# A transformer block's forward and backward: the DMA transposes replaced by TensorE transposes

## The chip, the cores and the metric

The kernel runs on one NeuronCore of a Trainium2 chip. A core has a matrix engine (TensorE, PE in the profile, with its weight loads listed as PEld), three engines for elementwise work (VectorE or DVE, ScalarE or ACT, GpSimd or POOL), and a queue engine for transfers (SyncE or SP). They run side by side, each in its own program order, and wait for each other by semaphores. Operands lie in SBUF, 128 partitions wide; TensorE writes its results to PSUM, from where DVE or ACT copies them out. The metric is the device time of one execution in microseconds; lower is better.

## What is computed

One transformer block with adaptive layer norm and all its gradients. S = 2048 tokens, D = 512, 32 heads of 16, a hidden layer of F = 1792; everything comes in and goes out as bf16.

```
mod = silu(c) @ w_mod                      -> sa, ca, ga, sb, cb, gb
h   = layernorm(x) * (1 + ca) + sa
q, k, v = split(h @ wqkv)                  32 heads of 16
x   = x + ga * (softmax(q k^T / 4) v) @ wo
h   = layernorm(x) * (1 + cb) + sb
out = x + gb * (relu(h @ w1 + b1)^2 @ w2 + b2)
...
returns out and the gradients of x, wqkv, wo, w1, b1, w2, b2, c, w_mod for grad_out
```

In the attention backward, for a head, with p the unnormalised exponentials of the transposed scores and dP the gradient that arrives at them, dS = p * dP. It is used twice: with its keys in the free dimension for dK (as it comes), and with its queries in the other place for dQ, which needs dS turned.

## The kernel before

**Stages.** `phase_fwd` (0 to 980 us) walks over four query chunks of 512, eight groups of four heads and two pairs of heads in each; a step is one block of 128 keys for one pair: two score matmuls into a PSUM tile of 1024 columns (L388), one exponential of it on ScalarE (L391), and eight small matmuls that multiply earlier exponentials with the values (L322). `last_chunk` (980 to 1166 us) does the output projection and the mlp of the last chunk and the weight gradients of the mlp (`gen_dw1`, `gen_dw2`). `phase5` with `attn_bwd` (1166 to 2376 us) is the attention backward, and `phase6` (to 2498 us) the gradients of wqkv, wo, x and the modulation.

**Background work in the forward.** Beside the steps runs other work, written as generators: `gen_qkv` projects q and k for the coming groups in the first chunk (one tile of 512 tokens of one group is a `gen_fm`), and from the second chunk on `gen_mlp` does everything that follows the attention of the chunk before: projection, layer norm, both mlp layers, their backward, and dO. A generator yields the cost of what it has issued, in units of a 512-column matmul. `Background.step` lets it run at a rate of 1.2 (first chunk) or 1.14 units a step; a yield of `("wait", n)` holds it for n steps, so that another engine or a transfer can finish. Some points must be reached by a deadline: `bg.until(mark)` runs the generator on without regard to rates or holds, for instance before a group's projections are needed, and at the end of the forward until the mark `fc2_2`. `bg.drain` does the same for what is left.

**Attention backward.** A unit is one block of 128 queries of one pair of heads (index `ib`, with `i = ib % 4`) against 512 keys (index `c`); there are 8 groups x 2 pairs x 4 x 16 = 1024. For each of the two heads of unit n the loop issues a score matmul (L1608, tile "st") and the dP matmul of unit n-1 (L1522, tile "dp"), the exponential (L1611, ScalarE), and dS = p * dP (L1526, VectorE). The score matmul and the dP matmul use different halves of the array's rows and run together. In 160 units the second half of dS goes over ScalarE and GpSimd instead (`dP_pool`, L1540 and L1541). Then come, in odd units, the four matmuls per unit of dK and dV (`kv`, L1459), and in even ones those of dQ (`dq`, L1484), which read dS turned. PSUM tiles come from pools: `stp` with three buffers for "st" (also for the turns), `dpp` with three for "dp". A new tile waits until the reader of the tile three before it in the same pool is done.

**The transposes before.** dS is collected for four units in a tile of 32 blocks of 128 x 128; after the fourth, SP issues one DMA transpose of it into a buffer `dsT` (L1549), and two such groups feed one round of `dq`. In one of four groups `turn_ds` (L1556 to L1566) turns the first four of the 32 blocks on TensorE instead. The same kind of transfer turns the projections into token-major form (L646), the values (L705), weights (L677, L1139, L1152, L1153), attention output and `grad_out` (L1176, L1178), the normalised input of the mlp (L1201), dx and dO (L1248, L1332), the mlp operands of the weight gradients (L946, L950), and dq, dk, dv in the tail (L1737). All are issued from SP and there are 416 of them.

Of the kernel before, what the change touches and what calls it, by code (L numbers as in the profile page):

```python
# [105 lines left out]
class K:  # L106
# [160 lines left out]
    def phase_fwd(self):  # L267
# [144 lines left out]
        self.gT_l = self.mk.tile([P, DT, 512], BF16, name="fT", bufs=2)  # L412
        nc.sync.dma_start_transpose(self.gT_l[:], self.io["grad_out"][0, S - 512:, :])
        x0s = []
# [209 lines left out]
    def gen_fm(self, ps, t, g, s0, dst=None, masked=None):  # L624
# [19 lines left out]
        def token_major():  # L644
            tm = eb.tile([P, 4, 4, 32], BF16, name="ev_tm")
            nc.sync.dma_start_transpose(tm[:].rearrange("p s j e -> p s (j e)"), dst)  # L646
            if t:
                nc.gpsimd.dma_start(self.ktm_d[g, :, s0:s0 + 512], tm[:].rearrange("p s j e -> p (s j e)"))
                return
            tmc = eb.tile([P, 4, 4, DH], BF16, name="ev_tmc")  # L650
            nc.gpsimd.tensor_copy(tmc[:], tm[:, :, :, 0:DH])
            w = 4 * DH
            nc.gpsimd.dma_start(self.qtm_d[g, :, s0 // P * w:(s0 // P + 4) * w],
                                tmc[:].rearrange("p s j d -> p (s j d)"))

        if self.late is None:
            token_major()
        else:
            self.late.append(token_major)
        yield 1  # L660

    def gen_qkv(self, kp):
# [3 lines left out]
        for g in range(1, NQ):  # L666
# [8 lines left out]
            if 3 < g <= 3 + self.DT:  # L675
                wt = self.qkv_eb.tile([P, 3 * self.DT, P], BF16, name="wm_t", bufs=1)
                nc.sync.dma_start_transpose(wt[:], w[:])  # L677
                nc.gpsimd.dma_start(self.WmT_d[g - 4], wt[:].rearrange("p n k -> p (n k)"))
# [14 lines left out]
    def gen_vt(self, s0):  # L693
# [4 lines left out]
        for k in range(4):  # L698
            vp = self.vpads[k]
            v = self.Vaug[:, s0 + k, :, 0:DH].rearrange("p (g j) d -> p g j d", j=4)  # L700
            one = self.qkv_eb.tile([P, 1], F32, name="one", bufs=2)
            nc.vector.memset(one[:], 1.0)
            nc.gpsimd.tensor_scalar(vp[:, :, 0:2, 0:DH], v[:, :, 2:4, :], one[:], 1.0, ALU.mult, ALU.mult)
            nc.gpsimd.tensor_scalar(vp[:, :, 2:4, 0:DH], v[:, :, 0:2, :], one[:], 1.0, ALU.mult, ALU.mult)
            nc.sync.dma_start_transpose(vT[:, :, k * P:(k + 1) * P], vp[:].rearrange("p g j e -> p (g j e)"))  # L705
            yield ("wait", 1)
        nc.gpsimd.dma_start(self.VTq_d.rearrange("g p s -> p g s")[:, :, s0 * P:(s0 + 4) * P], vT[:])

    def by_quad(self, t):
# [52 lines left out]
    def last_chunk(self, bg, O_b, x0s, o32):  # L762
# [10 lines left out]
        tm_v = lambda t: t.rearrange("(st p) d -> p st d", p=P)[:, st0:st0 + 4, :]  # L773
        tps = self.open_pool("tps", bufs=2, space=PSUM)
        e0 = self.open_pool("e0", bufs=1)
# [22 lines left out]
        for k in range(4):  # L798
            turn(O_b[:, k, :], DT, OT[:, k], "scalar" if k % 2 else "vector")
        bg.take(4)  # L800
        stats = mk.tile([P, 4, 6], F32, name="stats")
        mv = mk.tile([P, 4, 2], F32, name="mv")
# [136 lines left out]
    def turned(self):  # L939

        nc, ST, FT = self.nc, self.ST, self.FT
        lasts = []

        def get(pool, src, src_d, ft):
            r = pool.tile([P, ST - 4, P], BF16, name="tm_blk", bufs=4)
            nc.sync.dma_start_transpose(r[:], src_d[ft, :, :(ST - 4) * P])  # L946
            if ft % 4 == 0:
                n = min(4, FT - ft)
                t = pool.tile([P, 4, 4, P], BF16, name="tm_l", bufs=2)
                nc.sync.dma_start_transpose(t[:, :n].rearrange("p f s k -> p (f s) k"),  # L950
                                            src[:, ft:ft + n, :].rearrange("p f k -> p (f k)"))
                lasts.append(t)
            return [r[:, st, :] for st in range(ST - 4)] + [lasts[-1][:, ft % 4, i, :] for i in range(4)]

        return get

    def gen_dw1(self, sb, xh2, duT):
# [21 lines left out]

        dus = [turned(sb, duT, self.duT_d, ft) for ft in range(3)]  # L980
        for ft in range(2):
            load(ft)
        yield 0
        for ft in range(FT):
            if ft + 3 < FT:
                dus.append(turned(sb, duT, self.duT_d, ft + 3))
            if ft + 2 < FT:
# [36 lines left out]
    def gen_dw2(self, sb, g_tm, aT, tb):  # L1024
# [14 lines left out]
        mods = {2: (3, self.dsb_col), 5: (4, self.dcb_col)}  # L1039
        load(0)  # L1040
        load(1)
        yield 0
        load(2)
        for ft in range(FT):
            if ft + 3 < FT:
                load(ft + 3)
            a, w2_blk = blks[ft]
# [73 lines left out]
    def gen_weights_1(self):  # L1121
# [14 lines left out]
        for kt in range(DT):  # L1136
            nc.gpsimd.tensor_scalar(w1[:, kt, :], w1[:, kt, :], self.opcbT[:, kt:kt + 1], 1.0, ALU.mult, ALU.mult)
            yield 0
        nc.sync.dma_start_transpose(self.wogaT[:].rearrange("p a b c -> p (a b) c"), wo[:].rearrange("p a b -> p (a b)"))  # L1139

    def gen_weights_2(self):
# [4 lines left out]
        for (a, b) in zip(cuts, cuts[1:]):  # L1146
# [4 lines left out]
            yield ("wait", 4)  # L1151
        nc.sync.dma_start_transpose(self.W2gbT[:].rearrange("p a b c -> p (a b) c"), w2[:].rearrange("p a b -> p (a b)"))  # L1152
        nc.sync.dma_start_transpose(self.W1mT[:].rearrange("p a b c -> p (a b) c"), w1[:].rearrange("p a b -> p (a b)"))  # L1153
        yield ("wait", 8)
# [13 lines left out]
    def gen_mlp(self, sc, O_b):  # L1168
# [4 lines left out]
        tm_v = lambda t: t.rearrange("(st p) d -> p st d", p=P)[:, st0:st0 + 4, :]  # L1173
        x_v, g_v, out_v = tm_v(io["A_x"][0]), tm_v(io["grad_out"][0]), tm_v(io["out_0"][0])
        OT = mk.tile([P, 4, DT, P], BF16, name="fT", bufs=2)
        nc.sync.dma_start_transpose(OT[:].rearrange("p a b c -> p (a b) c"), O_b[:].rearrange("p a b -> p (a b)"))  # L1176
        gT = mk.tile([P, DT, 512], BF16, name="fT", bufs=2)
        nc.sync.dma_start_transpose(gT[:], io["grad_out"][0, s0:s0 + 512, :])  # L1178
        yield ("wait", 9 if sc else 14)
        x1 = mk.tile([P, 4, D], F32, name="x1")  # L1180
# [19 lines left out]
        xhT = mk.tile([P, 4, DT, P], BF16, name="fT", bufs=2)  # L1200
        nc.sync.dma_start_transpose(xhT[:].rearrange("p a b c -> p (a b) c"), xh[:].rearrange("p a b -> p (a b)"))  # L1201
        nc.gpsimd.dma_start(tm_v(self.xhat2_d), xh[:])
# [29 lines left out]
        for k in range(4):  # L1232
# [14 lines left out]
            dxT = mk.tile([P, DT, P], BF16, name="dxT", bufs=2)  # L1247
            nc.sync.dma_start_transpose(dxT[:], dxb[:])  # L1248
            todo.append((k, dxT))
# [39 lines left out]
    def gen_do(self, sc, k, dxT, pads=None, o32=None):  # L1289
# [41 lines left out]
        c0 = k % 2 * P  # L1331
        nc.sync.dma_start_transpose(self.dOTq[:, :, c0:c0 + P], dOpad[:].rearrange("p g j e -> p (g j e)"))  # L1332
        if k % 2:
# [97 lines left out]
    def attn_bwd(self):  # L1431
# [17 lines left out]
        masked, kvs = self.masked, self.kvs  # L1449
        pend, pendq, turnq, two = [], [], [], []  # L1450
        own = dT_free[-1]
# [91 lines left out]
        def dS(u):  # L1543

            (T, g, jp, c, ib, kvT, pu, dsg, i, grp) = u
            pend.append((T, g, jp, c, ib, kvT, pu, dsg[:, i]))
            if i == G - 1:
                dsT, n = grp
                nc.sync.dma_start_transpose(dsT.rearrange("p (b k) -> p b k", k=P)[:, n:, :],  # L1549
                                            dsg[:].rearrange("p i a k -> p (i a k)")[:, n * P:])  # L1550
                two.append(dsT)
                if len(two) == 2:
                    pendq.extend((T, g, jp, c, ib - 2 * G + 1, a, sub, two[:]) for a in range(2) for sub in range(4))
                    two.clear()

        def turn_ds(dsg, grp, skip, late):  # L1556

            dsT = next(t for t in dT_free if not late or t is not own)
            dT_free[:] = [t for t in dT_free if t is not dsT]
            grp.extend((dsT, 0 if skip else 4))  # L1560
            if skip:
                return
            tp = stp.tile([P, 4, P], BF16, name="st")
            for b in range(4):
                nc.tensor.transpose(tp[:, b, :], dsg[:, 0, 0, b * P:(b + 1) * P], self.ident[:])
            nc.scalar.copy(dsT[:, 0:4 * P], tp[:].rearrange("p b k -> p (b k)"))  # L1566

# [4 lines left out]
        for g in range(NQ):  # L1572
            for jp in range(2):
# [16 lines left out]
                for c in range(SC):  # L1590
                    c0 = 512 * c
                    for ib0 in range(0, ST, G):
# [6 lines left out]
                        for i in range(G):  # L1599
# [19 lines left out]
                            if i % 2 == 1 and len(pend) >= 4:  # L1619
                                kv_two(1 if odd(c, ib) else 2)  # L1620
                            elif i % 2 == 0 and len(pendq) > 2 * G:
                                for _ in range(4 if end else 2):
                                    dq(pendq.pop(0))
                            if i == 2:
                                turn_ds(dsg, grp, no_turn(c, ib), end and m > 2)
            T = Tn
        with tc.manual_schedule(engines=ALL):
# [3 lines left out]
            for a in range(2):  # L1631
                dP(last, a)
            dS(last)
            while len(pend) > 2:
                kv_two()
# [49 lines left out]
    def phase6(self):  # L1685
# [47 lines left out]
        def load_a(i):  # L1733
            s2 = order[2 * i]
            dqT = wk.tile([P, 3, 2, DT, P], BF16, name="dqT", bufs=3)
            for t in (1, 2, 0):
                nc.sync.dma_start_transpose(dqT[:, t].rearrange("p s n k -> p (s n) k"),  # L1737
                                            parts[t][:, s2:s2 + 2, :].rearrange("p s d -> p (s d)"))
            dx1s = [wk.tile([P, D], F32, name="dx1_6", bufs=6) for _ in range(2)]
# [226 lines left out]
```

## Time and profile before

| | us |
|---|---|
| time, median of 3 runs | 2512.6 (2509.9 to 2517.3) |
| profiled execution, its own time | 2500.3 |
| its span | 2498.5 |

The page's first two lines of totals, and its row of the span in 40 slices, where a digit is the busy share in tenths and PEclk the clock that TensorE was granted:

```profile
PE 2410.2 (96%) x26211; PEld 1061.6 (42%) x26439; DVE 1695.0 (68%) x3487; ACT 2283.1 (91%) x3757; POOL 753.5 (30%) x1337
## 2 busy tenths in 40 slices
PE   8999999999999999999999999999999999999998
PEld 4555555555555555583233332333333333333343
DVE  6222322422332343576999999999999999999957
ACT  7999999999999997534999999999999999999945
POOL 2344531220131022245222323322333222322223
PEclk9999999999999999999999999999999999999999
DMA  4589661541243045499999999999999999999997
```

A busy TensorE is not one at its peak, since the ends of its matmuls are modelled; what bounds a stage has to be read from that stage. The forward is slices 1 to 15, the last chunk 16 to 18, the attention backward 19 to 38. A row of the page's groups gives the line, the engine, what is written and read with its shape, the count, then busy time and mean duration of one (ns), and the idle time just before it with what ended it.

### The profile page before, as it was taken

The page shows a single profiled execution, that of the slowest core. Times are in us where ns is not written, and L with a number is a line of the kernel's source. Part 1 is how long each engine was busy: PE and PEld are TensorE (multiplying, and loading weights), DVE is VectorE, ACT ScalarE, POOL GpSimd, SP SyncE. Part 2 cuts the span into 40 slices and gives each one's busy share as a digit, 9 for nine tenths or more (in the row PEclk, how much of TensorE's full clock was granted, in tenths as well). Part 3 has the DMA queues.
Part 4 walks back from the last instruction along what each step waited for, and adds up shares of the span by engine and source line. Part 5 has one row for each costly group of instructions (what it writes and reads, how often), then busy time and mean ns, then how long its engine had stood idle before and what let it go on. Part 6 is the DMA issues. An engine that isn't in the chain of part 4 may idle for free.

```text
span 2498.5 us, 67897 instructions
## 1 busy us (share of the span) xinstructions
PE 2410.2 (96%) x26211; PEld 1061.6 (42%) x26439; DVE 1695.0 (68%) x3487; ACT 2283.1 (91%) x3757; POOL 753.5 (30%) x1337
## 2 busy tenths in 40 slices
PE   8999999999999999999999999999999999999998
PEld 4555555555555555583233332333333333333343
DVE  6222322422332343576999999999999999999957
ACT  7999999999999997534999999999999999999945
POOL 2344531220131022245222323322333222322223
PEclk9999999999999999999999999999999999999999
DMA  4589661541243045499999999999999999999997
GB/s 166 135 179 208 169 125 47 132 100 40 92 114 98 23 123 147 110 199 216 232 235 233 232 227 231 237 234 231 230 235 239 234 230 236 234 233 236 238 217 192
DMA packets 1293547, 454.13 MB, mean 182 GB/s; under 512 B 1236948, under 2 KB 1261398, under 8 KB 1293222
## 3 DMA queue, kind: packets, MB, share of 16 engines
q1 hardware_dynamic: 1252422, 344.68, 71.8%
q0 software_dynamic: 38720, 104.04, 13.9%
q8 instruction: 207, 3.39, 0.6%
q10 hardware_dynamic: 2080, 1.05, 0.2%
q14 instruction: 118, 0.97, 0.1%
HBM read 75.83 MB, written 64.49 MB: 56 GB/s over the span
## 4 chain that ended last, share of the span: by engine, by line
PE 49%; ACT 35%; DMA 7%; issue 5%; DVE 3%; POOL 1%; SPq 1%; ACTq 0%; DVEq 0%; POOLq 0%
ACT pu L391 26%; PE st L1608 17%; PE acckv L1459 8%; ACT pu L1611 6%; DMA dsT<-ds 5%; PE accq L1484 5%; PE st L388 4%; PE dp L1522 2%; PE accbank L322 2%; PE dps L1050 2%; PE dp L1659 1%; PE st L1754 1%; ACT csq L1540 1%; PE pps L1237 1%; DVE ds L1526 1%
## 5 line engine op out<-in xcount | busy, mean ns | idle before, releaser
L1526 DVE TENSOR_TENSOR ds<-dp,pu 128x512 bf16<-128x512 f32 x1888 | 1166.0, 682 | 34.6 <-PE dp L1522 19.1
L1611 ACT ACTIVATE pu<-st 128x512 bf16<-128x512 f32 x2048 | 1073.8, 666 | 34.7 <-PE st L1608 21.3
L391 ACT ACTIVATE pu<-st 128x1024 bf16<-128x1024 f32 x992 | 912.1, 1077 | 4.2 <-PE st L388 3.7
L388 PE MATMUL st<-QTm,KTq 128*128 128x512 bf16 x1859 | 560.9, 377 | 27.1 <-ACT pu L391 6.1
L322 PEld LDWEIGHTS <-pu 128*128 128x128 bf16 x8192 | 346.7, 96 | 236.1 <-issue 3.0
L1522 PE MATMUL dp<-kvm,q 64*128 64x512 bf16 x1024 | 365.0, 384 | 2.0 <-DVE ds L1526 0.7
L322 PE MATMUL accbank<-Vaug,pu 128*128 128x17 bf16 x8192 | 357.4, 171 | 8.3 <-ACT Vaug L522 1.1
L1522 PE MATMUL dp<-kvm,dOTg 64*128 64x512 bf16 x1024 | 363.6, 383 | 0.3
L1608 PE MATMUL st<-kvm,q 64*128 64x512 bf16 x1024 | 349.4, 382 | 5.4 <-ACT pu L1611 0.2
L1608 PE MATMUL st<-kvm,QTg 64*128 64x512 bf16 x1024 | 348.1, 381 | 6.5
L1541 POOL TENSOR_TENSOR ds<-csq,pu 128x512 bf16<-128x512 f32 x128 | 147.2, 1150 | 627.0 <-ACT csq L1540 553.6
L388 PEld LDWEIGHTS <-KTq 128*128 128x128 bf16 x1984 | 188.4, 96 | 176.9 <-issue 124.8
L1459 PE MATMUL acckv<-ds,Qg 128*16 128x512 bf16 x1024 | 176.2, 382 | 0.3
L1459 PE MATMUL acckv<-pu,q 128*16 128x512 bf16 x1024 | 176.3, 383 | 0.0
L1459 PE MATMUL acckv<-ds,q 128*16 128x512 bf16 x1024 | 176.2, 383 | 0.0
L1459 PE MATMUL acckv<-pu,dOg 128*16 128x512 bf16 x1024 | 176.0, 382 | 0.0
L302 POOL DMA_DIRECT2D QTm<-QTq_d x124 | 63.1, 511 | 341.5 <-PE st L388 320.0
L1608 PEld LDWEIGHTS <-q 64*128 64x128 bf16 x1024 | 67.0, 94 | 163.5 <-issue 150.6
L1608 PEld LDWEIGHTS <-QTg 64*128 64x128 bf16 x1024 | 67.1, 94 | 160.6 <-issue 145.7
L329 DVE RECIPROCAL rl<-accbank 128x4 f32<-128x4 f32 x128 | 22.9, 179 | 158.3 <-PE accbank L322 158.2
L1522 PEld LDWEIGHTS <-q 64*128 64x128 bf16 x1024 | 88.8, 93 | 52.9 <-issue 43.3
L1522 PEld LDWEIGHTS <-dOTg 64*128 64x128 bf16 x1024 | 88.2, 93 | 52.9 <-issue 43.8
(390 smaller groups left out, 3055.1 us busy)
## 6 DMA issues: line engine op xcount, KB each, us to landing
KTq<-KTq_d POOLq DMA_DIRECT2D x24, 512.0 KB, 3.9
duT_d<-auT POOLq DMA_DIRECT2D x3, 1792.0 KB, 7.9
aT_d<-rT POOLq DMA_DIRECT2D x3, 1792.0 KB, 11.5
KTq_d<-KTq SPq DMA_DIRECT2D x32, 128.0 KB, 2.1
QTq_d<-ev_fm SPq DMA_DIRECT2D x32, 128.0 KB, 4.3
ktm_d<-ev_tm POOLq DMA_DIRECT2D x32, 128.0 KB, 2.5
VTq_d<-vT POOLq DMA_DIRECT2D x4, 1024.0 KB, 6.3
dx<-dx_d SPq DMA_DIRECT2D x16, 256.0 KB, 4.6
```

What stands on the lines that cost most here:

```text
L302: nc.gpsimd.dma_start(QTm[j][32 * j:32 * j + 32, :], self.QTq_d[g, 32 * j:32 * j + 32, 512 * qc:512 * (qc + 1)])
L322: nc.tensor.matmul(acc[:, a, sub, :], lhsT=pu[:, a, sub * P:(sub + 1) * P], rhs=Vaug[:, kb, h, :], start=(kb == 0 and a == 0 and sub == 0) ...
L388: nc.tensor.matmul(stt[:, a, :], lhsT=KT[:, kb * P:(kb + 1) * P], rhs=QTm[2 * jp + a][:], start=True, stop=True)
L391: nc.scalar.activation(pu[:], stt[:], ACT.Exp, scale=self.scale)
L1050: nc.tensor.matmul(pt[:], lhsT=a[st], rhs=g_tm[:, st, :], start=(st == 0), stop=(st == ST - 1))
L1459: nc.tensor.matmul(acckv[r:r + DH, :], lhsT=T[n][:, ib, col:col + DH], rhs=src[:, a, :], start=(ib == 0), stop=(ib == ST - 1))
L1484: nc.tensor.matmul(accq[r:r + 32, o:o + 256], lhsT=T["K"][:, 4 * c + sub, col:col + 32], rhs=v[:, r // 32 % 2 * 2:r // 32 % 2 * 2 + 2, 4 * ...
L1522: nc.tensor.matmul(dp[:], lhsT=T["dOT"][rd, ib * P:(ib + 1) * P], rhs=masked["VT"][a][rd, 512 * c:512 * (c + 1)], start=True, stop=True)
L1526: nc.vector.tensor_tensor(dsg[:, i, a], dp[:], pu[:, a, :], ALU.mult)
L1541: nc.gpsimd.tensor_tensor(dsg[:, i, 1], f[:], pu[:, 1, :], ALU.mult)
L1608: nc.tensor.matmul(stt[:], lhsT=T["QT"][rs, q], rhs=masked["KT"][a][rs, c0:c0 + 512], start=True, stop=True)
L1611: nc.scalar.activation(pu[:, a, :], stt[:], ACT.Exp, scale=self.scale)
```

## The change

Every DMA transpose is replaced by transposes on TensorE: the block is loaded as the stationary operand, the identity streams past it, the result lands in PSUM in bf16, eight blocks of 128 x 128 to a PSUM tile, and is copied to its place in SBUF. A helper `gen_turn` does this, with a yield of 1.5 units after four blocks and after each tile; `turn_now` is the same without yields. The copies are made by VectorE where nothing else is said, and by ScalarE and VectorE in turn for dS, for the weight gradients' operands and for dq, dk, dv.

- dS: each unit is turned by itself, eight blocks, one unit after its dS was issued (`turn_unit`); the PSUM tile is an "st" tile of the pool `stp`, the copy is ScalarE's for even `i`, VectorE's for odd. `turn_ds` goes, and dQ starts one group earlier (`len(pendq) > G`).
- Forward: `gen_fm`, `gen_vt`, `gen_qkv`, `gen_mlp`, `gen_do`, `gen_weights_1` and `gen_weights_2` turn through `gen_turn` with tiles of the pool `mps`, and get holds in front of the turns in which an operand is not ready at once.
- Weight gradients: the operands come by a plain transfer into one staging buffer (`tm_st`), and are turned at the next request.
- `grad_out` is loaded plainly and turned from SBUF; in the last chunk it is turned by `last_chunk`'s own `turn`.

```diff
-            nc.sync.dma_start_transpose(tm[:].rearrange("p s j e -> p s (j e)"), dst)
+            self.turn_now(tm[:].rearrange("p s j e -> p s (j e)"), dst, 4)
...
-        if self.late is None:
-            token_major()
-        else:
+        if self.late is not None:
             self.late.append(token_major)
-        yield 1
+            yield 1
+            return
+        yield ("wait", 1)
+        token_major()
+        yield 1.5
...
+    def gen_turn(self, dst, src, n, pool=None, name="pps", copies=None):
+
+        nc = self.nc
+        for b0 in range(0, n, 8):
+            m = min(8, n - b0)
+            pt = (pool or self.mps).tile([P, 8, P], BF16, name=name)
+            for i in range(m):
+                nc.tensor.transpose(pt[:, i, :], src[:, (b0 + i) * P:(b0 + i + 1) * P], self.ident[:])
+                if i == 3:
+                    yield 1.5
+            (copies or [nc.vector.tensor_copy])[b0 // 8 % len(copies or [0])](dst[:, b0:b0 + m, :], pt[:, :m, :])
+            yield 1.5
+
+    def turn_now(self, *a, **k):
+        for _ in self.gen_turn(*a, **k):
+            pass
...
         def get(pool, src, src_d, ft):
-            r = pool.tile([P, ST - 4, P], BF16, name="tm_blk", bufs=4)
-            nc.sync.dma_start_transpose(r[:], src_d[ft, :, :(ST - 4) * P])
+            flush()
+            g = pool.tile([P, (ST - 4) * P], BF16, name="tm_st", bufs=1)
+            nc.sync.dma_start(g[:], src_d[ft, :, :(ST - 4) * P])
+            r = pool.tile([P, ST - 4, P], BF16, name="tm_blk", bufs=3)
+            todo.append((r[:], g[:], ST - 4))
...
         xhT = mk.tile([P, 4, DT, P], BF16, name="fT", bufs=2)
-        nc.sync.dma_start_transpose(xhT[:].rearrange("p a b c -> p (a b) c"), xh[:].rearrange("p a b -> p (a b)"))
+        yield ("wait", 3)
+        yield from self.gen_turn(xhT[:].rearrange("p a b c -> p (a b) c"), xh[:].rearrange("p a b -> p (a b)"), 4 * DT)
...
             dxT = mk.tile([P, DT, P], BF16, name="dxT", bufs=2)
-            nc.sync.dma_start_transpose(dxT[:], dxb[:])
+            yield ("wait", 3)
+            yield from self.gen_turn(dxT[:], dxb[:], DT)
...
-        nc.sync.dma_start_transpose(self.dOTq[:, :, c0:c0 + P], dOpad[:].rearrange("p g j e -> p (g j e)"))
+        yield ("wait", 4)
+        yield from self.gen_turn(self.dOTq[:, :, c0:c0 + P], dOpad[:].rearrange("p g j e -> p (g j e)"), NQ)
...
             pend.append((T, g, jp, c, ib, kvT, pu, dsg[:, i]))
+            tq.append(u)
+
+        def turn_unit(u):
+
+            (T, g, jp, c, ib, kvT, pu, dsg, i, grp) = u
+            if not grp:
+                late = (g, jp) == (NQ - 1, 1) and c * SC + ib // G > 2
+                grp.append(next(t for t in dT_free if not late or t is not own))
+                dT_free[:] = [t for t in dT_free if t is not grp[0]]
+            dsT = grp[0]
+            self.turn_now(dsT.rearrange("p (b k) -> p b k", k=P)[:, 2 * G * i:2 * G * (i + 1), :],
+                          dsg[:, i].rearrange("p a k -> p (a k)"), 2 * G, pool=stp, name="st",
+                          copies=[(nc.scalar.copy, nc.vector.tensor_copy)[i % 2]])
             if i == G - 1:
-                dsT, n = grp
-                nc.sync.dma_start_transpose(dsT.rearrange("p (b k) -> p b k", k=P)[:, n:, :],
-                                            dsg[:].rearrange("p i a k -> p (i a k)")[:, n * P:])
                 two.append(dsT)
...
-                            elif i % 2 == 0 and len(pendq) > 2 * G:
+                            elif i % 2 == 0 and len(pendq) > G:
                                 for _ in range(4 if end else 2):
                                     dq(pendq.pop(0))
-                            if i == 2:
-                                turn_ds(dsg, grp, no_turn(c, ib), end and m > 2)
+                            while len(tq) > 1:
+                                turn_unit(tq.pop(0))
...
             for t in (1, 2, 0):
-                nc.sync.dma_start_transpose(dqT[:, t].rearrange("p s n k -> p (s n) k"),
-                                            parts[t][:, s2:s2 + 2, :].rearrange("p s d -> p (s d)"))
+                self.turn_now(dqT[:, t].rearrange("p s n k -> p (s n) k"), parts[t][:, s2:s2 + 2, :].rearrange("p s d -> p (s d)"),
+                              2 * DT, pool=stp, name="st", copies=[(nc.scalar.copy, nc.vector.tensor_copy)[t % 2]])
```

## The prediction

> **What bounds the kernel now.** I read the table of stretches first, then the costliest groups, then the transposes that TensorE (PE) already makes, last the timeline. The stretches (columns: stretch, its length, busy us and instructions of PE, PEld, DVE, ACT, POOL, granted PE clock, DMA share, GB/s) are opening, forward, last chunk, backward loop and tail:
>
> ```profile
> 64.00:301.00 237.00, 223.02 (x2774) 129.04 (x2822) 61.12 (x160) 235.29 (x257) 107.98 (x192) 1.00 0.76 177
> 301.00:980.00 679.00, 656.23 (x8027) 370.88 (x8176) 217.05 (x646) 676.48 (x738) 150.67 (x242) 1.00 0.36 91
> 980.00:1166.50 186.50, 177.09 (x1539) 111.43 (x1547) 117.01 (x463) 73.30 (x171) 80.70 (x118) 0.99 0.79 184
> 1166.50:2376.00 1209.50, 1187.38 (x12772) 371.30 (x12772) 1174.66 (x1904) 1194.02 (x2427) 355.64 (x680) 1.00 1.20 232
> 2376.00:2498.50 122.50, 111.10 (x596) 49.80 (x603) 83.16 (x208) 56.33 (x114) 39.32 (x69) 0.98 0.86 205
> ```
>
> In the forward ACT alone is full. In the backward loop ACT (99%), PE (98%) and DVE (97%) all are, and so are the DMA engines (share 1.20); only POOL has room. The loop is 1024 units in 1209.5 us, 1.18 us each. Its work per unit, from the groups:
>
> ```profile
> L1526 DVE TENSOR_TENSOR ds<-dp,pu 128x512 bf16<-128x512 f32 x1888 | 1166.0, 682 | 34.6 <-PE dp L1522 19.1
> L1611 ACT ACTIVATE pu<-st 128x512 bf16<-128x512 f32 x2048 | 1073.8, 666 | 34.7 <-PE st L1608 21.3
> ```
>
> The idle before each is small: nobody waits long. The removed operation, in the view of its line, issues 256 transfers, 7.2 us each to land, and is waited for by PE 8.5 us in 1209.5:
>
> ```profile
> L1549 SPq DMA_TRANSPOSE dsT<-ds x208: 3490/4262/6457, 1173.4 to 2377.8; - x104
> L1549 SPq DMA_TRANSPOSE keep<-ds x48: 3550/4204/5392, 1192.2 to 2300.7; - x48
> ...
>   PE accq L1484: 8.5, 13
> ```
>
> So the change takes nearly nothing off the path, and puts its work on the engines that are full.
>
> **Prices.** The trace has PE transposes with both kinds of copy (tile view of last_chunk's turn; min/median/max in ns):
>
> ```profile
> L782 PE MATMUL tp<-ident,dOpad x32: 219/219/229, 1039.9 to 1061.0; 128*128 128x128 bf16 x32
> L783 DVE COPY fT<-tp x4: 414/418/424, 983.2 to 997.6; 128x512 bf16<-128x512 bf16 x4
> ...
> L783 ACT COPY dOTq<-tp x4: 1003/1012/1012, 1040.8 to 1061.3; 128x1024 bf16<-128x1024 bf16 x4
> ```
>
> And it has the loop's own four-block turn among its neighbours:
>
> ```profile
> 1606.05 0.38 PE L1608 MATMUL st<-kvm,q 64*128 64x512 bf16 x1
> ...
> 1606.44 0.29 PE L1484 MATMUL accq<-dsT,keep 128*32 128x256 bf16 x2
> ...
> 1606.78 0.40 PE L1565 MATMUL st<-ident,ds 128*128 128x128 bf16 x4
> ...
> 1607.11 0.39 PE L1608 MATMUL st<-kvm,q 64*128 64x512 bf16 x1
> ...
> 1607.22 0.62 ACT L1566 COPY dsT<-st 128x512 bf16<-128x512 bf16 x1
> ...
> 1607.69 1.13 ACT L1611 ACTIVATE pu<-st 128x512 bf16<-128x512 f32 x2
> ```
>
> Four transposes take 0.40 us of which 0.22 is the last one's length, so they start 0.06 apart (in the records 0.056); start to the next matmul, with the change of array tiling, is 0.33. Eight take 0.33 + 4 x 0.056 = 0.55, from first start to end 0.62. The exponentials of 512 columns follow each other at 0.48 (two in 1.13, the last being 0.65), so ACT's slot is 0.48 for 512 columns; for 1024 I take 0.91, the pace of the forward's L391 (912.1 us / 992 = 0.92). DVE's copy of 1024 bf16 is in no row: from 418 ns for 512 (about 0.15 fixed, the rest 1.9 columns a ns) 0.69 us.
>
> Two rules of the Trainium skill stand against rows. "TensorE: Matmul & The Clock Gate", Part 4: PE-mode transpose, gives some 275 ns per transpose inside a kernel and says it does not count toward releasing the clock. By that 8 would cost 2.2 us a unit, the loop 1.8 ms more; the records' 0.056 us between starts makes it 0.45. The 219 ns are latency, and the clock stayed at 1.00 in the loop, though with few transposes. I take the row. "VectorE: DVE Perf Modes", Rules for kernel authors, tells one to accept 1x on PSUM sources; its cycle table then makes 1024 columns 1.19 us (estimate). The 418 ns for 512 are below 1x, so 0.69 it is; 1.19 is kept as a rival.
>
> **Backward loop.** The built program has 8,192 PE transposes of dS, eight per unit, and 1024 copies of 1024 columns, 512 on ACT (even units), 512 on DVE. Work per pair of units: PE 1.9 to 2.2 (its matmuls in the timeline) + 2 x 0.55 = 3.0 to 3.3; ACT 4 x 0.48 + 0.91 = 2.83 and its small copies; DVE 4 x 0.60 + 0.65 = 3.05, less what POOL takes.
>
> That is not yet the pace. Pool stp has three PSUM buffers and each unit now draws three tiles (st, st, turn), so each buffer gets a fixed job and PE loses its lead on ACT: the second st of unit n+1 waits for the second exponential of unit n, and a turn for the copy of the turn before it. On ACT the even copy stands before the next unit's two exponentials. The ring over two units: second st of an even unit to dq 0.31; dq to first transpose 0.33; eight transposes 0.62; to the copy 0.06; copy 0.91; exponential 0.48; second exponential to its end 0.63; to the next even unit's second st 0.05 (PE follows ACT at that distance in the forward). Sum **3.39 us a pair**, longer than any engine's work; ACT stands idle some 0.5 of it. The DVE copy fits: it starts 3.06 after the ring's start and ends at 3.75, the turn that waits for it is due at 4.0.
>
> 512 x 3.39 = 1736. Added: 160 units send half their dS through ACT and POOL (1150 ns each, L1541), which now must end before that unit's turn, +0.31 each, 50; 48 turns of dk, dv and dq, 0.7 each, 33; 64 kvT copies, mostly in ACT's idle, 10. Sum 1829. My hand sums fall short of the real loop: for before, ACT's rows give 1149 (977 exponentials, 77 + 36 + 31 + 28 copies) where 1209.5 passed, 5%. I add half of that, 48. Loop 1877, **+667**.
>
> **Forward.** It keeps to ACT's 0.917 us a step while the background stays within its rate. Each projection tile now costs a hold and half a unit more, and in the first query chunk no longer fits: the program forces the rest out between steps, eleven blocks in the built order: four of four or five tiles, seven of about two. A forced tile is 4 matmuls (0.65 to the last start), 1.18 to the end of its DVE cast (0.38 + 0.06 + 0.69 + 0.05), 0.22 for four transposes: 2.05 with ACT idle. 4 x 9.4 + 7 x 3.7 less the 3 that before has: **+60**. In the later chunks the turns (48 units and 31 held steps each) make the mlp late by about 67 of 256 steps a chunk, so that nearly all of chunk 2's mlp is left at the last step and runs with no exponential beside it: first layer 56 x 0.216 = 12.1, xhT 1.8; du 14 x 1.05 by DVE = 14.7 + 1; then four tiles with their norm chain on DVE, which was hidden:
>
> ```profile
> 942.92 0.70 DVE L1273 BATCH_NORM_STATS2 lnd_st<-pps 128x6 f32<-128x512 f32 x1 [3.20 <-PE pps L1237]
> ...
> 946.17 0.43 DVE L1244 CAST dxb<-dx 128x512 bf16<-128x512 f32 x1
> ```
>
> The last matmul started at 942.51 and the cast ends at 946.60: 4.1, of which PE waits 3.9. A tile: 3.0 + 3.9 + 0.2 = 7.2; its dO, 0.86 + 3.5 (DVE, 946.59 to 949.83) + 0.45 = 4.8. 4 x (7.2 + 4.8) + fc2 3.2 = 51. Sum 81 less before's 2: **+79**. Norm chains that outlast their holds: about 4, left out.
>
> **Last chunk and tail.** 448 transposes of the weight gradients at 0.056 in a stretch where PE is the bound: 25; their loads now go through one staging buffer: 3.9 us to landing (row for 512 KB) against 3.6 + 0.7 of PE a tile, so hidden; 23 fc2 units more, 5; gT 1: **+31**. Tail: 192 transposes, 11, and changes 2; the last dS transfer (12.5 us in the chain of waits) goes, of which I count 6, for other matmuls lie beside it: **+7**. W2gbT, W1mT and woga: PE work within the forward's rate, counted in its lateness.
>
> Sum: 667 + 60 + 79 + 31 + 7 = 844 on the profiled execution's 2500.3: 3344. The median of the runs shown is 12 higher, so **3350 us**, 33% slower.
>
> **Rivals.** (1) *The engines overlap fully*: queues absorb the ring, and the loop goes at ACT's work: 1149 - 31 + 466 = 1584, times 1.05: 1667, +458; 3150. For it: ACT is 99% busy in before with the same order of work. Against it: three tiles on three buffers. (2) *DVE's copy at 1x*: 1.19 us ends at 4.25, the even turn slips 0.28 a pair, and DVE's work becomes 3.6 a pair: 512 x 0.3 = 150; 3500. (3) *Transposes at 275 ns or a gated clock*: 9,680 x 0.22 = 2100; 5450. (4) *Not slower*: the dS transfers are the bound, not the engines; the chain of waits has them at 5% (125 us), the DMA share is 1.20, and without them 2500 - 125 = 2375. It decides only if ACT's added work per unit stays below its idle, 1.2% of 1.18 us or 0.015, against 0.45 added; and PE's measured wait is 8.5, not 125. (5) *The change doesn't do this*: excluded by the built order, where SP has no transposes left.
>
> **Chances.** Mine 0.75; (1) 0.13; (2) 0.09; (3) 0.02; (4) 0.01. Mine alone is 3240 to 3470 (ring 3.2 to 3.6). The range reaches (1) and beyond (2): 3140 to 3560. A change of 0.3% is about what can be told from none here; faster 0.01, same 0.01, slower 0.98.
>
> **What would show it.** Loop length near 1880 with ACT below 90% busy and its idle ended by PE's turns; PE's st waiting for ACT; the DVE copy at 0.69; DMA share far below 1; eleven gaps in ACT before 310 us, and some 80 us after the last exponential of the forward with DVE and PE taking turns. Wrong if ACT stays at 97% or more (rival 1), the copies differ, or transposes start more than 0.06 apart.

## The result and the profile after

The changed kernel takes **3308.9 us** (median of 4 runs, 3305.1 to 3313.3) where the kernel before took 2511.2 on the same chip (4 runs, 2507.2 to 2517.3): a ratio of 1.317, interval 1.314 to 1.321. The profiled execution's span is 3303.3 us, 804.8 more than before.

The table of stretches of the changed kernel, with the columns of the prediction's first table: the first chunk from 64 us, the later chunks to the last exponential of the forward (at 1043.7), a new stretch behind it, the last chunk, the backward loop from its first to its last exponential, and the tail:

```profile
64.00:301.00 237.00, 198.31 (x2444) 117.94 (x2485) 79.29 (x199) 174.15 (x189) 78.11 (x147) 1.00 0.23 75
301.00:1043.70 742.70, 703.82 (x8909) 415.60 (x9072) 215.26 (x611) 737.84 (x805) 158.45 (x253) 1.00 0.21 67
1043.70:1138.50 94.80, 62.43 (x285) 27.16 (x286) 60.25 (x154) 1.06 (x2) 20.68 (x33) 0.82 0.29 93
1138.50:1367.30 228.80, 208.77 (x2001) 138.22 (x2013) 129.57 (x495) 109.57 (x209) 80.71 (x119) 0.99 0.43 136
1367.30:3163.00 1795.70, 1747.64 (x20708) 830.55 (x20707) 1540.83 (x2414) 1688.87 (x2873) 357.45 (x680) 1.00 0.05 13
3163.00:3303.30 140.30, 124.77 (x787) 61.88 (x795) 89.61 (x218) 72.27 (x131) 38.78 (x69) 0.97 0.38 121
```

Four things are to be seen. In the first chunk ACT is busy 174 of 237 us, 235 before. The third row is work that had hardly existed as a stretch of its own: ACT busy 1 us of 95, PE and DVE 62 and 60, so they take turns, and the granted clock falls to 0.82. In the loop the DMA share is 0.05 (1.20 before), all three engines have more to do, and DVE is no longer full (86%). In the tail nothing but the length stands out.

By the same boundaries in both traces, the stages account for all of it. The profiled execution of before was 11 us faster than its median, so the profiles are 805 us apart and the medians 798.

| stage | before | after | more | forecast |
|---|---|---|---|---|
| forward, to its last exponential | 979.5 | 1043.7 | 64 | 60 |
| from there to the last chunk | 2.8 | 94.9 | 92 | 79 |
| last chunk, to the loop's first exponential | 184.6 | 228.7 | 44 | 31 |
| loop, first to last exponential | 1208.9 | 1795.9 | 587 | 667 |
| tail | 122.6 | 140.1 | 17 | 7 |
| sum | | | 805 | 844 |

The waits of the first chunk (64 to 301 us), and those of the stretch behind the forward; after the waiting engine and line and what it waited for: us, times, longest:

```profile
ACT pu L391 <- PE st L388: 61.3, 12, 10.5
```

```profile
PE pps L717 <- DVE dxb L1278: 16.4, 4, 5.1
PE pps L717 <- DVE dOpad L1360: 13.7, 4, 3.4
```

Ten of the 12 waits are forced projection blocks (the other two are 0.5 us each), and an eleventh block follows at 304.5 us: in the trace the distance of two exponentials is 9.1 us once, 11.6 three times and 4.3 to 4.8 seven times, where a step takes 0.92. The eight waits of 3.4 to 5.1 us are the norm chain and the dO chain of the third chunk's mlp, each now with a turn at its end for which PE waits.

### The profile page after: what moved, and what is told of

The parts are those of the page before. It is cut to its first block, busy times and chain, and to the rows that moved or that the text cites. A ratio compares the mean times of both kernels' runs of the same rounds, so it can differ in the third digit from the quotient of the medians.

```text
span 3303.3 us, 86819 instructions
## 1 busy us (share of the span) xinstructions
PE 3101.7 (94%) x35635; PEld 1620.8 (49%) x35879; DVE 2156.8 (65%) x4195; ACT 2831.5 (86%) x4259; POOL 753.4 (23%) x1337
## 4 chain that ended last, share of the span: by engine, by line
PE 50%; ACT 35%; issue 10%; DVE 3%; DMA 1%; POOL 1%; ACTq 0%; POOLq 0%; DVEq 0%; SPq 0%
ACT pu L391 21%; PE st L717 13%; PE st L1642 12%; ACT pu L1645 8%; PE accq L1520 4%; PE acckv L1495 4%; ACT dsT L720 3%; PE st L388 3%; PE accbank L322 1%; PE st L1790 1%; PE pps L630 1%; PE dp L1695 1%; PE dps L1080 1%; PE dps L1024 1%; ACT csq L1576 1%
## 5 line engine op out<-in xcount | busy, mean ns | idle before, releaser
L1562 DVE TENSOR_TENSOR ds<-dp,pu 128x512 bf16<-128x512 f32 x1888 | 1228.6, 685 | 203.3 <-PE dp L1558 155.3
L1645 ACT ACTIVATE pu<-st 128x512 bf16<-128x512 f32 x2048 | 1127.1, 611 | 53.1 <-PE dp L1558 17.0
L717 PE MATMUL st<-ident,ds 128*128 128x128 bf16 x8192 | 645.8, 220 | 17.6 <-ACT dsT L720 3.1
L717 PEld LDWEIGHTS <-ds 128*128 128x128 bf16 x8192 | 487.1, 97 | 303.5 <-issue 266.0
L388 PE MATMUL st<-QTm,KTq 128*128 128x512 bf16 x1823 | 552.7, 377 | 37.3 <-ACT pu L391 3.9
L720 ACT COPY dsT<-st 128x1024 bf16<-128x1024 bf16 x416 | 427.0, 1026 | 50.1 <-PE st L717 38.1
L1642 PE MATMUL st<-kvm,QTg 64*128 64x512 bf16 x1024 | 364.2, 382 | 15.0 <-ACT dsT L720 6.5
L1642 PE MATMUL st<-kvm,q 64*128 64x512 bf16 x1024 | 363.6, 381 | 13.5 <-ACT dsT L720 6.1
L720 DVE COPY dsT<-st 128x1024 bf16<-128x1024 bf16 x416 | 287.7, 691 | 42.7 <-PE st L717 32.4
```

The source lines that it names most:

```text
L388: nc.tensor.matmul(stt[:, a, :], lhsT=KT[:, kb * P:(kb + 1) * P], rhs=QTm[2 * jp + a][:], start=True, stop=True)
L717: nc.tensor.transpose(pt[:, i, :], src[:, (b0 + i) * P:(b0 + i + 1) * P], self.ident[:])
L720: (copies or [nc.vector.tensor_copy])[b0 // 8 % len(copies or [0])](dst[:, b0:b0 + m, :], pt[:, :m, :])
L1562: nc.vector.tensor_tensor(dsg[:, i, a], dp[:], pu[:, a, :], ALU.mult)
L1642: nc.tensor.matmul(stt[:], lhsT=T["QT"][rs, q], rhs=masked["KT"][a][rs, c0:c0 + 512], start=True, stop=True)
L1645: nc.scalar.activation(pu[:, a, :], stt[:], ACT.Exp, scale=self.scale)
```

## Experiments

**1. Which part costs what.** The first kernel is the one before with only the loop's `attn_bwd` and the helper `gen_turn` of the changed one; the second is the changed kernel with the loop of before.

```diff
             if i == G - 1:
-                nc.sync.dma_start_transpose(dsT.rearrange("p (b k) -> p b k", k=P)[:, n:, :],
-                                            dsg[:].rearrange("p i a k -> p (i a k)")[:, n * P:])
...
-                            if i == 2:
-                                turn_ds(dsg, grp, no_turn(c, ib), end and m > 2)
+                            while len(tq) > 1:
+                                turn_unit(tq.pop(0))
```

This is the core of the first kernel's edit; the second kernel has it backwards.

> The kernel before with one part of the change alone: dS turned by TensorE in the backward loop, all other transposes by DMA as before. The loop went from 1209.5 to 1799 us with the whole change. Theory A (the stages add up): the loop is 1790 to 1800 us again and the time 2511 + 589 - 8 (the last dS transfer) = 3092 us. Rival: the loop's length owes something to what the forward leaves to it, or the forward's DMA transposes were slowed by nothing that dS does: then the time lies more than 30 us from 3092.

> The changed kernel with dS turned by DMA as before, all other transposes on TensorE. Theory A: what is left of the change outside the loop, 3309 - 2511 - 581 = 217 us, so 2728 us, with the loop at 1209 us. Rival: the dS transfers need the DMA engines that the other transposes leave free, or lengthen the tail: more than 30 us off.

Measured: only dS 3087.7 us (ratio 1.231, 1.228 to 1.233), all but dS 2729.9 (1.088, 1.085 to 1.090). Against the 2508.9 of before measured beside them these are +578.8 and +220.9, together 799.7; the whole change is +797.6. The parts add up, so the stages may be judged nearly alone. The loop of the first kernel takes 1794.8 us and that of the second 1218.8 (ten more than in the fast execution of before that was profiled); the second has the same 64, 92 and 45 us in front of the loop as the changed kernel. The two tails tell more: with dS turned on TensorE and dq, dk, dv by DMA it is 121.9 us, the other way round 144.2. So the last dS transfer was worth 0.7 us where dq, dk and dv go by DMA and 4.1 where they are turned, and their turns cost 21.6 us beside that transfer and 18.2 without it.

**2. What sets the loop's pace, from above.** Four more transposes a unit, into PSUM that the copy reads anyway: in odd units (DVE's copy), where the ring of the prediction doesn't pass, and in even ones (ACT's copy), where it does (`i % 2 == 0` in the line below).

```diff
-            for b in range(8):
+            for b in [*range(8)] + ([*range(4)] if i % 2 == 1 else []):
                 nc.tensor.transpose(pt[:, b, :], src[:, b * P:(b + 1) * P], self.ident[:])
```

> The changed kernel with twelve instead of eight transposes in the odd units (the first four blocks are turned twice into the same place); the even units, whose copy is ScalarE's, stay at eight. 512 x 4 x 0.056 = 115 us of PE more. Theory R (the ring of second score, dq, turn, ScalarE copy and two exponentials sets the pace of two units; the odd turn is not on it): the loop grows by less than 40 us. Theory P (PE's own stream of matmuls and changes of tiling sets the pace, about 3.2 to 3.3 of 3.5 us a pair): it grows by 90 to 115 us, time 3400 to 3425.

> The same in the even units, whose turn is on the ring. Theory R: 512 x 0.224 = 115 us more, all of it. Theory P: 90 to 115 us more, as for the odd ones. Together with the odd one: R has only this one grow, P both alike.

Measured: odd 3365.0 us (1.341, 1.339 to 1.344), even 3389.3 (1.351, 1.348 to 1.354). The loops grew by 57.7 and 80.6 us for 115 us of added PE work each. Neither theory holds for the whole loop: PE's time counts half off the ring and 70% on it. The table behind the next experiment shows that this average mixes pairs that behave differently.

**3. The same from below.** Both copies shortened to 512 columns (the first 64 units keep full copies), or four transposes and full copies.

```diff
-            (nc.scalar.copy, nc.vector.tensor_copy)[i % 2](dst, pt[:])
+            n = 8 if (g, jp) == (0, 0) else 4
+            (nc.scalar.copy, nc.vector.tensor_copy)[i % 2](dst[:, :n, :], pt[:, :n, :])
```

```diff
-            for b in range(8):
+            for b in range(4):
                 nc.tensor.transpose(pt[:, b, :], src[:, b * P:(b + 1) * P], self.ident[:])
-            (nc.scalar.copy, nc.vector.tensor_copy)[i % 2](dst, pt[:])
+            (nc.scalar.copy, nc.vector.tensor_copy)[i % 2](
+                dst.rearrange("p (h b) k -> p h (b k)", h=2),
+                pt[:, :4, :].rearrange("p b k -> p (b k)").unsqueeze(1).to_broadcast([P, 2, 4 * P]))
```

> The changed kernel, with both engines' copies of a turned unit shortened from 1024 to 512 columns after the first 64 units (eight transposes as before; half of the turned dS is left out of the copy, so dQ reads older values there). The loop of the changed kernel, first to last exponential, took 1795.9 us. Theory R (the ring through ScalarE's copy sets the pace, 3.39 us a pair): the ring loses 0.91 - 0.48 = 0.43 us a pair, until TensorE's own work (3.2 to 3.3 a pair) is the bound: the loop falls by 100 to 130 us, time 3180 to 3210. Theory P (TensorE's own stream sets the pace, it was almost without gaps): the loop falls by less than 30, time above 3280. Theory M (the two are equal to within their jitter and each is the bound in some units, as the two runs with longer turns suggest, which cost half and two thirds of what was added): 40 to 90 less, time 3220 to 3270.

> The changed kernel, with four transposes a unit in place of eight and the copies as long as before (the copy reads the four turned blocks twice, so half of the turned dS is left out of dQ). TensorE's work falls by 4 x 0.056 = 0.22 us a unit, 230 us in 1024 units; the ring by 0.22 us a pair, 115 us. Theory R (ring): loop 115 us shorter, time near 3195. Theory P (TensorE's stream): 170 to 230 shorter, until ScalarE's work is the bound, time 3080 to 3140. Theory M (both in turn): the mirror image of the two runs with longer turns, which added 58 + 81: about 140 shorter, time near 3170.

Measured: half copies 3219.5 us (1.283, 1.278 to 1.289), half turns 3214.5 (1.281, 1.276 to 1.285). Both loops fell by about the same, to 1708.6 and 1705.8. Their rows in the table of stretches, loop only (busy PE, PEld, DVE, ACT, POOL):

```profile
1367.30:3076.60 1709.30, 1673.07 (x20712) 800.22 (x20710) 1439.15 (x2414) 1485.82 (x2874) 356.57 (x680) 1.00 0.05 14
```

```profile
1372.80:3078.60 1705.80, 1562.64 (x16625) 658.98 (x16623) 1516.17 (x2414) 1674.64 (x2873) 356.80 (x681) 1.00 0.05 13
```

For the half copies theory M has the size (87, in 40 to 90); the half turns missed all three numbers (90; the nearest is R's 115).

With short copies PE is busy 98%, which looks like PE's own stream, 1.67 us a unit. It isn't, for PE still waits:

```profile
PE st L1597 <- POOL ds L1577: 26.9, 119, 0.4
```

That is POOL's product in the units whose second half of dS goes over ScalarE and POOL; the fifth transpose of the odd turn waits for it. A busy share hides part of such waits, since a matmul's record is longer than its distance to the next. So they are counted here by starts: where a PE instruction starts later than is usual at its place, and within 75 ns of the semaphore that it waited for, the lateness is a wait, and the rest is PE's own stream (estimates from the traces, us):

| loop | changed | odd 12 | even 12 | half copies | half turns |
|---|---|---|---|---|---|
| PE's own stream | 1644 | 1756 | 1758 | 1637 | 1410 |
| PE's waits | 152 | 98 | 119 | 72 | 295 |

The stream moves nearly as the edits say (+115, +115, 0, -230), so it is 1.60 us a unit or 3.2 a pair, and no loop is at its stream. Of the 152 us, 81 go to exponentials, 55 to ACT's copies of turned tiles, 14 to POOL's product, and less than 3 to all of DVE's work, so PE is not held up by DVE. With half copies POOL's product has 47 of the 72.

The mean pair also hides that there are several kinds (mean distance between the first exponentials of two even units, us):

| pairs | number | changed | odd 12 | even 12 | half copies | half turns |
|---|---|---|---|---|---|---|
| first pair of a group of four units | 256 | 3.26 | 3.40 | 3.50 | 3.19 | 3.10 |
| second pair, with a half of dS over POOL, no other extra | 128 | 3.61 | 3.84 | 3.61 | 3.61 | 3.44 |
| the others, most with a turn of dk, dv, dq or a copy of kvT | 127 | 3.90 | 3.85 | 4.07 | 3.37 | 3.69 |

In the first pairs the longer even turn counts in full (0.23 us for the 0.22 added), as the ring has it. In the 128 pairs with POOL neither that nor shorter copies change anything, while a longer odd turn counts in full: there a third chain sets the time, from dP through ACT's copy and POOL's product (1.15 us) to the odd turn, and neither theory had it. The half turns are no clean test of the ring, since they turn only the first head's half and so also take away the wait for POOL's product. So the loop is set in part by the ring and in part by this chain. Why the odd turn costs 0.14 in the first pairs is not shown; PE's own stream, 3.2 a pair in the mean, is near their 3.26.

**4. The stretch behind the forward: who made the mlp late.** First the mlp's five turns given back to DMA; then all turns kept and the background's rate raised.

The first edit is shown for `grad_out`; OT, xhT, dxT and dOTq have it likewise.

```diff
-        for k in range(4):
-            yield from self.gen_turn(gT[:, :, k * P:(k + 1) * P], g_s[:, k, :], DT)
+        nc.sync.dma_start_transpose(gT[:], io["grad_out"][0, s0:s0 + 512, :])
```

```diff
-                rate = 1.14 if qc else 1.2
+                rate = 1.4 if qc else 1.2
```

> The changed kernel, with the five turns of the mlp in the forward (attention output, grad_out, normalised input, dx, dO) given back to DMA transposes with the holds of the kernel before; the turns of the projections, values and weights, of the last chunk, of dS and of the tail stay on TensorE. Theory of the prediction (the mlp's turns make the mlp late, and what is left of it runs with no exponential beside it): the block after the last forward exponential, 92 us, goes to a few us; the first chunk's 61 us of gaps stay; time 3215 to 3235. Rival (the mlp is late because the first chunk and the turned weights push it back, or would be exposed anyway): the block keeps more than 60 of its 92 us, time above 3275.

> The changed kernel, with the background's rate in the later three query chunks raised from 1.14 to 1.4 units a step, so that the mlp with its turns is not late. Theory L (the exposed block is the planner's: the price of the turns in units does not fit into its rate, though the engines could take them): the 92 us at the end of the forward go to below 15, the steps get longer by at most 40 us in all, time 3235 to 3270. Rival E (TensorE is full in those steps, so its 60 us of work in that block must be paid wherever it is put): the block shrinks but the steps grow by as much or more, time 3285 to 3330.

Measured: mlp by DMA 3241.9 us (1.292, 1.287 to 1.296), rate 3278.4 (1.306, 1.302 to 1.311). By DMA the stretch falls from 94.9 to 17.0 us: the mlp's turns made it, as forecast. The sum came out 7 us above the expected range, since the last exponential of the forward came 11 us later (one wait of PE for the transfer of the attention output, 3.1 us, and two gaps in the first chunk that were 3.8 longer together, of which more below; the rest is open) and the last chunk took 6 more, which was not followed up. The rate moved 39 us out of the stretch (55.4 left) and lengthened the steps by 12.5: the planner's rate was part of it, and engine time was to be had at a third of the price. What kept the rest for the end, holds or chains, was not tested. Neither L nor E had the size.

**5. The fallen clock.** Matmuls into an unread tile, where PE waits for DVE in the third chunk's mlp.

```diff
+            if sc == SC - 2:
+                wp = mps.tile([P, 512], F32, name="pps")
+                for _ in range(14):
+                    nc.tensor.matmul(wp[:], lhsT=self.ones_b[:], rhs=rT[:, 0, :], start=True, stop=True)
             dxT = mk.tile([P, DT, P], BF16, name="dxT", bufs=2)
             yield ("wait", 3)
...
+        if sc == self.SC - 2:
+            wp = self.mps.tile([P, 512], F32, name="pps")
+            for _ in range(12):
+                nc.tensor.matmul(wp[:], lhsT=self.ones_b[:], rhs=dOp_t[:], start=True, stop=True)
         yield ("wait", 4)
```

> The changed kernel, with matmuls into an unread PSUM tile while TensorE waits for VectorE in the mlp of the third chunk: 14 of 512 columns after each dx tile and 12 after each dO tile (output unchanged). In the block after the last forward exponential the granted clock fell to 0.68 in 1090 to 1138.5, and 14 dx matmuls took 4.7 to 5.1 us, 3.0 in the forecast's sum. Theory C (the fallen clock is why this block took 92 us and not 79): the block takes 78 to 84 us, the clock stays above 0.9, the dx matmuls take 3.0 to 3.3, time 3295 to 3301. Rival W (the waits for VectorE's norm chain alone set it, and matmuls that fill them delay the next group as much as the clock gains): the block stays at 88 to 96, time 3305 to 3313.

Measured: 3299.6 us (3297.6 to 3303.3; 1.314, 1.312 to 1.315), which the intervals don't quite part from the changed kernel's 1.314 to 1.321. The traces do: the stretch fell from 94.9 to 89.9 us and its clock rose from 0.82 to 0.94:

```profile
1043.90:1133.80 89.90, 79.82 (x394) 34.51 (x390) 59.89 (x153) 1.12 (x2) 20.63 (x33) 0.94 0.30 97
```

Two groups of dx matmuls in the changed kernel, and the same two with the fillers:

```profile
1080.67 4.69 PE L1271 MATMUL pps<-W1mT,auT 128*128 128x512 bf16 x14
1097.00 5.06 PE L1271 MATMUL pps<-W1mT,auT 128*128 128x512 bf16 x14
```

```profile
1082.30 3.19 PE L1271 MATMUL pps<-W1mT,auT 128*128 128x512 bf16 x14
1098.97 3.19 PE L1271 MATMUL pps<-W1mT,auT 128*128 128x512 bf16 x14
```

All four groups of 14 dx matmuls (first start to last end) took 3.19, 4.69, 5.06 and 4.21 us in the changed kernel and 3.19 each with the fillers. From the first dx matmul to the end of the last turn of dO it was 62.7 us and is now 56.5; some 1.5 us were lost before the first filler. So theory C has the cause of the slow matmuls, the clock, the time and about half the gain; the stretch itself, 89.9, lies where rival W had it (88 to 96). The fillers also cost something, one group of 12 having run at the low clock for 4.84 us with the next turn behind it.

**6. A small dose, from the kernel before.** Its 64 half turns taken away, or 256 of them (`False` in the place of `True`).

```diff
-                                turn_ds(dsg, grp, no_turn(c, ib), end and m > 2)
+                                turn_ds(dsg, grp, True, end and m > 2)
```

> The kernel before, with its 64 half turns of dS on TensorE (four blocks each, copied by ScalarE) taken out: all dS goes by DMA transpose. Theory R (a turned unit costs the same wherever it is, 587 us / 1024 units of two halves = 0.29 us a half): 64 x 0.29 = 18 us less, 2490. Theory A (each half costs ScalarE its slot of 0.48, since ScalarE is 99% busy): 31 us less, 2478. Rival D (the DMA transposes are themselves near a bound in the loop of before, share 1.20, and the half turns were there to relieve them): no change or slower, 2505 to 2540.

> The kernel before, with a half turn on TensorE (four blocks, ScalarE's copy of 512 columns) in all 256 groups instead of 64. Theory R (0.29 us a half, as on the average of the whole change): 192 x 0.29 = 55 us more, 2564. Theory A (ScalarE's slot of 0.48 each): 92 us more, 2600. Rival D (the shorter DMA transposes pay for it): within 10 us of before.

Measured: none 2545.2 us (1.013, 1.011 to 1.015), 256 halves 2576.4 (1.025, 1.024 to 1.027). Both are slower than before. With none the loop takes 1241.4 us (1208.9 before) although ACT and PE have less to do, and in the view of the dS transfers those who wait for them are:

```profile
  PE accq L1484: 45.9, 49
```

Before it was 8.5 us in 13 waits; a transfer now lands 7.7 us after issue (7.2), the DMA share is 1.26 (1.21). Rival D is right on that side. With 256 the loop takes 1280.9, 0.375 us for each half added, between theories R and A. Of the three doses measured (0, 64 and 256 half turns) the kernel before has the best; no version here beats it.

## Why the prediction was right, and where its terms were off

Forecast 3350, measured 3309; the mechanism holds: the work goes to engines that were full, and next to nothing pays for it. That the total is so near is in part luck, since the loop was forecast 80 us too long and the other stages together 40 too short.

**Loop, +667 against +587.** The prices are those of the rows. Transposes start 0.056 us apart. ACT's next instruction starts 0.905 after a copy (0.91 assumed). The DVE copy of 1024 columns, in the page's groups of the changed kernel, is

```profile
L720 DVE COPY dsT<-st 128x1024 bf16<-128x1024 bf16 x416 | 287.7, 691 | 42.7 <-PE st L717 32.4
```

691 ns against 0.69. Rival 2 had read the row "accept 1×" of the Trainium skill's "VectorE: DVE Perf Modes" too widely: the tier table of the same page lets a copy that reads PSUM run at up to 2×, and its cycle table then makes 0.66 us of 1024 columns (an estimate), near what was measured. The 275 ns of the skill's "TensorE: Matmul & The Clock Gate" (Part 4) are no price here: the starts of 8,192 transposes lie 0.056 us apart, and the granted clock of the loop was 1.00 in the mean, with matmuls between the transposes.

The ring can be seen in ACT's timeline of one pair:

```profile
2000.02 1.04 ACT L720 COPY dsT<-st 128x1024 bf16<-128x1024 bf16 x1
2000.92 2.36 ACT L1645 ACTIVATE pu<-st 128x512 bf16<-128x512 f32 x4
2003.42 1.01 ACT L720 COPY dsT<-st 128x1024 bf16<-128x1024 bf16 x1
2004.33 0.60 ACT L1645 ACTIVATE pu<-st 128x512 bf16<-128x512 f32 x1
```

Copy to copy is 3.40 us, as worked out (3.39); each copy delays the next exponentials by 0.9. The mean pair takes 3.51.

Two sizes were off. The **half of 5%** added for what hand sums miss, 48 us, was not needed: without it the sum is 1829, 33 above the measured 1796. Those 33 lie in the **ring of the first pairs**: the 256 of them take 3.26 us in the mean where 3.39 was assumed; why was not followed up. The additions came out at the forecast 93 us by luck: against the 18 second pairs that have neither extra, a half over POOL costs 0.22 (0.31 assumed), and the turns and kvT copies cost 0.53 in 109 pairs, 58 us in all where 43 was assumed. PE's work "3.0 to 3.3 a pair" holds, 3.2 by its starts. The forecast had added the half over POOL to the ring; in the 128 pairs it is a chain of its own that sets the time in place of the ring (experiment 3).

The sign foretold as "ACT below 90% busy" did not show: the profile has 94%. Its busy time counts a copy as 1.026 us, though ACT starts the next instruction after 0.905. By starts (2048 exponentials at 0.49, 512 copies at 0.905, 160 small copies at 0.466 and the rest) ACT is taken 1609 of 1796 us, 90%, and idle 0.37 a pair where 0.5 was foretold. The shares alone would have spoken for rival 1; its time, 1667 for the loop, was not reached even with half the copies or half the turns.

**Forward, +60 against +64.** Right in kind and number: four long and seven short gaps, as foretold.

**Stretch behind the forward, +79 against +92.** Right in cause (experiment 4). The sum's tile of 3.0 + 3.9 and its dO of 4.8 took the clock as full. In the trace the dx groups at the low clock are 4.4 us longer in all, the dO matmuls 2.0 (1.91 against 1.03 for four, twice, and 1.24), the turns about 2; a wait for the transfer of dx adds 1.3. Together these are some 10 of the 13; experiment 5 gives back 6.2. The term mis-sized is PE's time per tile.

**Last chunk, +31 against +44; tail, +7 against +17.** In the last chunk PE's busy time grew by 33 us (175.6 to 208.7), near the 31 of the sum, and its idle time by 11 (9 to 20), which had been counted as nothing. The longest of PE's waits there are for DVE's copies of turned blocks and for one load of 384 KB through the single staging buffer, both taken as hidden:

```profile
PE tp L717 <- DVE tm_blk L720: 7.2, 5, 2.8
PE tp L717 <- DMA tm_st<-duT_d: 3.7, 1, 3.7
```

In the tail both terms were wrong: the dS transfer gave back 0.7 to 4.1 us instead of 6, and the turns cost 18 to 22 instead of 13 (experiment 1).

**Rival 4** was dismissed rightly for the whole change, and for too simple a reason. That PE waits only 8.5 us for dS does not show that the transfers have room: experiment 6 takes away 64 half turns, 3% of the blocks, and loses 33 us. The kernel before had both the DMA engines and the elementwise engines at their edge.

## What to carry to other kernels

Where an engine-side replacement meets engines that are already full, price it from rows of the trace by distances between starts, not by durations or busy shares, and look for the ring that the new copies close through the PSUM buffers. Do it for each kind of iteration: here one ring fitted the plain pairs, another chain set those with a detour over POOL, and the mean of the loop showed neither. The ring's sum needed no further allowance for idle time here. A stall-free resource isn't one with room: a small step back and a small step forward on the kernel before tell where it stands.

## What the chip did that was not expected

A forced block of projections in the first chunk, the same instructions in two kernels with the same code up to there, ran at two clocks. The stretch 283.5 to 301 us of the changed kernel and of the half-turns kernel:

```profile
283.50:301.00 17.50, 12.21 (x129) 6.67 (x130) 6.97 (x13) 6.97 (x9) 6.87 (x14) 1.00 0.36 118
```

```profile
283.50:301.00 17.50, 12.23 (x62) 5.51 (x62) 5.85 (x11) 1.99 (x3) 5.41 (x11) 0.58 0.31 103
```

The granted clock is 1.00 in one and 0.58 in the other, 512-column matmuls of the block start 0.215 and 0.43 us apart, and the gap between two exponentials is 11.6 and 16.6 us. In the kernel with the mlp by DMA the clock there was 0.80, the gap 14.1. In all three PE's first wait in the block is 1.9 us, for POOL, and the others are 0.8 to 1.4, for a cast; why the clock was taken away in two of them and not in the third is open. In the stretch behind the forward, with waits of 3.4 to 5.1 us, it fell in the changed kernel, and filling the waits raised it (experiment 5).
